# Keys of the first batch through a hardware queue in float32, cast on the chip, and a new order of all steps

## The chip, the cores and the metric

The kernel runs on one core of a Trainium2 chip. The metric is the device time of one execution in microseconds. The core has five engines with instruction queues of their own: PE (TensorE, matmuls), DVE (VectorE), ACT (ScalarE), POOL (GpSimd) and SP (SyncE). Each works through its own queue in order, and semaphores hold an instruction back until its inputs are there. Transfers between memory and the core's own memory (SBUF) run on 16 DMA engines. They are fed by three queues here: POOL's, the software queue, which can also change a type on the way, and the hardware queues of SP and ACT. Matmul results land in PSUM, which holds eight tiles of this kernel at a time.

## What is computed

Attention over a small learned memory, and then a channel mix with weights. All shapes are fixed: 8 batches, 8 heads, 576 tokens, head size 64, 32 memory slots, and a mix of 512 to 1024 and back.

```python
a = softmax(phi, axis=2)                              # over the 576 tokens
k_m = einsum('bhsm,bhsd->bhmd', a, k)                 # 32 slots a head
v_m = einsum('bhsm,bhsd->bhmd', a, v)
attn = softmax(matmul(q, k_m^T) / 8)                  # over the 32 slots
x = matmul(attn, v_m)                                 # heads side by side: 512 wide
x_prev = x moved down by one token (zeros first)
xk = mu_k * x + (1 - mu_k) * x_prev
xr = mu_r * x + (1 - mu_r) * x_prev
kk = maximum(xk @ w_k, 0)
out = sigmoid(xr @ w_r) * ((kk * kk) @ w_v)
```

## The kernel before

The whole order of work is written out by hand in `PLAN`, a list of words, and each word is one step. The kernel's last loop goes through the words and records the instructions of each step, so a word's place sets its instructions' places in the queue of every engine that it uses. Nothing moves them afterwards. A word has a batch number (`0:s0`), or one of these heads:

- `p:` a load through POOL's queue: `p:q:0h` is the second half (heads 4 to 7) of batch 0's queries, `g` the first half, `p:k:1` all keys of batch 1, `p:wk:0-4` half of the weights `w_k`. `PRE` has the loads that come before everything else; `id` there builds the identity matrix on POOL.
- `c0:` to `c8:` keys of one group of tokens (L533): four matmuls of `w_k` with `xk`, relu on ACT (L540) or, with a `v` at the end, on DVE (L538), and the square on DVE (L545). Group 0 is batch 0 in two parts, `a` (320 tokens) and `b` (256); the others have 512.
- `g:` gate matmuls of one tile of 128 tokens (L561) and an exp on ACT (L566), `sg:` the rest of the sigmoid for two tiles (L572, L573), `o:` the output (L587), its product with the gate on DVE (L589) and the store on SP's queue.

The steps of a batch, in the order in which data flows through them:

- `exp`: the exponential of phi on ACT (L216); for batch 0 in two halves, `exp0` and `exp1`.
- `z`: sums of it over the tokens on PE (L240), and their reciprocal on DVE (L243).
- `kg0`, `kg1` for batch 0, `k`, `v`, `kv` later: `k_m` and `v_m` on PE (L230). A half needs its keys, and its half of `exp`.
- `nk` (DVE, L267) or `ak` (ACT, L265): the scaling of `k_m`. `tk`: its transposition on PE (L295) and the copy back on DVE (L300).
- `q0`, `q1`: the two halves of the queries transposed on DVE (L313). `s`, or `s0` and `s1`: scores on PE (L328) and their exponential on ACT (L333). Either part of the scores reads both halves of the queries.
- `l`, `h`, `y` or `fe`, `fs`, `fo`, `w`: two ways to divide by the softmax's sum. The first sums on PE (L343), takes a logarithm and an exponential on ACT (L348, L353) and multiplies on DVE (L377). The second does all on DVE.
- Batches 0 and 1 fold mu into `v_m` (`nm`, `nk0`, `nr0`, L425 and L437) and get `xk` and `xr` by matmuls (`mk`, `mr`, L286) with four copies each, two on ACT and two on DVE (L454). Later batches form `x` (`x0`, `x1`, copies on ACT, L389) and mix it on DVE (`dd`, `k0d`, `r2d`, L401 to L415), or in part on ACT (`r0e`, L412).

`mub` and `mu` need the two mu rows, `mu2`, which SP loads at the very start (L117, L118). `mub` spreads them by two matmuls on PE (L191) and two copies on DVE (L194, L195) for batches 0 and 1. `mu` is a small transposition (L199) with a DVE instruction (L200), for the later batches. `busyN` are N matmuls on zeros whose result nobody uses (L184): fillers, while PE has nothing else.

Phi of batch 0 comes through ACT's queue (L105). Queries, keys and values are float32 in memory and bfloat16 in SBUF, so POOL's queue casts them on the way; each has two buffers (`qs`, `kvs`), used by even and odd batches.

Of the kernel before, what the change touches and what calls it, by code (L numbers as in the profile page):

```python
# [10 lines left out]
F32 = mybir.dt.float32  # L11
# [5 lines left out]


PLAN = [
    "0:busy17 0:exp0 p:q:0g 0:q0 0:mub 0:exp1 0:z 0:kg0 0:busy7_1 p:k:0h 0:kg1 0:busy2_2 0:nk p:q:0h 0:q1 0:tk",  # L20
    "0:busy3_3 0:s0 p:v:0g 0:s1 0:busy2_4 0:l1 0:h1z 0:l3 0:busy2_5 p:v:0h 0:y1 0:vg1 0:h3z 0:y3 0:l0 0:l2 0:vg0",
    "0:busy3_6 0:nm1 0:nm0 0:h2z 0:y2 0:h0z p:wk:0-4 0:y0 0:mk1 0:mk0 c0:2b 0:mr1 c0:1b p:wk:4-8 c0:5a c0:0av p:phi:1",
    "c0:4bv c0:5bv 1:exp c0:4a c0:3a 0:mr0 1:z c0:3b c0:2a p:wr:0-4 c0:6b g:3 c0:0b c0:7av g:2 sg:1 0:mu p:k:1 1:k",
    "1:nk p:q:1 1:q1 1:q0 g:1 g:0 1:tk c0:1av 1:s c0:7bv c0:6a 1:l0 p:wv:0-2 1:h0z o:3a 1:l3 1:l2 1:h2z 1:l1 1:y0",
    "o:2a 1:h3z 1:y2 p:v:1 1:v 1:nk1 1:nk0 1:nr1 1:y3 1:h1z 1:y1 sg:0 o:0a p:wv:2-4 o:1a 1:mk0 p:phi:2 o:1b 2:exp",
    "o:3b 1:mk1 1:nr0 o:2b p:v:2 p:k:2 c1:2 c1:5v 1:mr1 c1:7 c1:4 2:z 2:kv 2:nk 1:mr0 p:q:2 2:q0 c1:3 2:av 2:tk 2:q1",
    "c1:1 c1:0 c1:6v 2:s o:0b 2:fe 2:fs 2:fo 2:w0 p:phi:3 3:exp p:v:3 p:phi:4 g:4 g:6 2:w1 g:5 3:z sg:2 o:4 o:5 4:exp",
    "2:x1 p:k:3 3:kv 3:nk 4:z 3:av p:q:3 2:x0 3:q1 g:7 3:q0 3:tk g:8 p:k:4 2:dd 2:k0d 3:s 2:k2d sg:3 o:6 3:l0 3:l3",
    "3:l2 2:r0d 3:l1 3:r0z 3:w0 o:7 3:r1z 3:w1 c2:4 c2:6 p:v:4 p:phi:5 c2:1 5:exp 2:r2d c2:3 c2:0 p:q:4 4:q1 4:kv",
    "4:av 4:q0 3:x0 c2:2 c2:5 4:ak p:q:5 c2:7 5:z 3:x1 3:dd 3:k2d g:11 g:10 sg:5 4:tk 5:q0 3:k0d 5:q1 g:9 o:11 o:10",  # L30
    "sg:4 o:8 3:r0e 4:s p:k:5 p:phi:6 p:v:5 5:kv 4:fe 4:fs 5:av 5:ak 3:r2e o:9 5:tk c3:7 6:exp c3:0 c3:3 4:fo c3:5",
    "5:s 5:fe 4:w1 4:w0 g:13 c3:2 c3:4 g:14 5:fs c3:1 p:q:6 4:x1 c3:6 6:z 5:fo 4:x0 4:dd 4:k0d 4:k2d 5:w1 g:15 p:q:7",
    "sg:7 g:12 sg:6 p:k:7 o:12 o:14 5:w0 p:phi:7 o:15 7:exp p:k:6 c4:5 c4:1 o:13 6:q1 7:z 6:q0 7:q0 4:r2e p:v:7 5:x1",
    "c4:7 p:v:6 6:kv 7:kv 7:nk 6:ak 6:av 5:x0 5:dd 4:r0e c4:6 6:tk c4:2 5:k0d g:16 g:17 5:k2d c4:0 c4:4 c4:3 7:q1 6:s",
    "6:fe g:19 6:fs 6:fo c5:3 g:18 c5:6 c5:1 sg:8 c5:5 7:nv 6:w0 6:w1 c5:0 5:r2e c5:2 o:17 sg:9 o:19 6:x1 o:16 c5:4v",
    "c5:7 6:x0 6:dd 6:k0d g:21 6:k2d 7:tk g:20 sg:10 o:21 o:20 5:r0e o:18 c6:7 c6:6 7:s 7:fe g:22 7:fs 7:fo c6:4 g:23",
    "sg:11 7:w1 g:26 c6:1v 7:w0 c6:5 6:r2e c6:3 c6:0 c6:2 o:23 7:x1 o:22 6:r0e 7:x0 7:dd g:25 7:k0d 7:k2d g:24 sg:12",
    "o:25 7:r2d g:27 sg:13 o:27 o:26 c7:1v o:24 c7:2 c8:2 c7:3 c8:3 c8:4v c7:0 c7:5v 7:r0e c8:5v g:29 c7:7 c7:6v",
    "c8:6v g:32 g:33 sg:16 g:28 c7:4v c8:0v sg:14 c8:7v o:28 c8:1 o:29 g:31 g:30 sg:15 o:30 o:33 o:31 g:34 g:35 sg:17",
    "o:34 o:32 o:35",  # L40
]

PRE = "k:0g id:"
SUMS = ()


NJ = 9
# [3 lines left out]
def kernel(  # L51
# [13 lines left out]
    nc = tc.nc  # L65
    B, H, S, D = q.shape
# [18 lines left out]
    work = ctx.enter_context(tc.sbuf_pool(name="work", bufs=2))  # L85
# [14 lines left out]
    def rows(src):  # L100
        return src.rearrange("h s d -> (h s) d").rearrange("(a p j) d -> p a (j d)", a=HH, j=NJ)

    def load_phi(b, eng):
        ph = ld.tile([128, HH, NJ, M], F32, name="ph", tag="ph")
        eng.dma_start(out=ph.rearrange("p h j m -> p h (j m)"), in_=rows(phi[b]))  # L105
        loads[b] = ph
# [5 lines left out]
        nc.gpsimd.dma_start(out=dst[r].rearrange("p h j d -> p h (j d)"), in_=rows(src)[r])  # L112

    load_phi(0, nc.scalar)
    nc.vector.memset(zeros, 0.0)  # L115
    mu2 = const.tile([2 * ND, 128], F32, name="mu2")
    nc.sync.dma_start(out=mu2[:ND, :], in_=moe_mu_k.rearrange("(a b) -> a b", b=128))  # L117
# [12 lines left out]
    def preload(word):  # L130

        what, _, part = word.partition(":")
        if what in weights:
            dst, src = weights[what]
            f0, f1 = (int(x) * 128 for x in part.split("-"))
            nc.gpsimd.dma_start(out=dst[:, :, f0:f1], in_=src[:, :, f0:f1])
        elif what == "id":
            make_identity(nc, identity)
        else:
            n = int(part[0])  # L140
            if what == "phi":
                load_phi(n, nc.gpsimd)
            else:
                dst = qs[n % 2].rearrange("p (h j) d -> p h j d", j=NJ) if what == "q" else kvs[n % 2][:, "kv".index(what)]
                src = {"q": q, "k": k, "v": v}[what][n]
                if part[1:] in ("g", "h"):
                    gs = slice(0, 2) if part[1] == "g" else slice(2, 4)
                    nc.gpsimd.dma_start(out=dst[:, gs].rearrange("p h j d -> p h (j d)"), in_=rows(src)[:, gs])  # L148
                elif part[1:]:
                    load_parity(dst, src, ROWS["ab".index(part[1])])  # L150
                else:
                    load_rows(dst, src)

    for word in PRE.split():
        preload(word)
# [46 lines left out]
    def attention(b):  # L202
        st = {}

        def ps_tile(shape, dtype, name):
            return psum.tile(shape, dtype, name=name, tag="ps", bufs=8)
# [5 lines left out]
        x0 = b * S % RING  # L212
        kv5, em = kvs[b % 2], ems[b % 2]

        def exp_phi(hs=slice(0, None)):
            nc.scalar.activation(em[:, :, hs].rearrange("p j h m -> p h j m"), loads[b][:, hs], AF.Exp)  # L216

        def ekv(parts, cs=(0, 1), gs=range(HH)):

            def go():  # L220
                w = parts.stop - parts.start
                kvps = st.get(("kvps", parts.start), {})
                kvps.update({c: ps_tile([128, w, D], F32, "kvps") for c in cs if c not in kvps})
                st["kvps", parts.start] = kvps
                for i in range(w):
                    st.setdefault("kv"[parts.start + i], {}).update({c: kvps[c][:, i, :] for c in cs})
                for j in range(NJ):
                    for g in gs:
                        for c in cs:
                            nc.tensor.matmul(kvps[c][g * M:(g + 1) * M], lhsT=em[ROWS[c], j, g, :],  # L230
                                             rhs=kv5[ROWS[c], parts, g, j, :],
                                             start=j == 0, stop=j == NJ - 1,
                                             skip_group_check=True)
            return go
# [68 lines left out]
        def q_tile():  # L303
            if "qT" not in st:
                st["qT"] = work.tile([128, HH, NJ * PB, 2], BF16, name="qT", tag="qT", bufs=2)
            return st["qT"]

        def turn_q(rows_, gs):

            def go():  # L310
                dst = q_tile()[rows_, gs].rearrange("p g n h -> p (g n h)")
                src = qs[b % 2][rows_, gs.start * NJ:gs.stop * NJ].rearrange("p n d -> p (n d)")
                nc.vector.transpose(dst.bitcast(U32), src.bitcast(U32))  # L313
            return go
# [127 lines left out]
        def mixed(w, hf):  # L442

            def go():
# [7 lines left out]
                for i in range(ND):  # L452
# [5 lines left out]
        steps = {"exp": exp_phi, "kv": ekv(slice(0, 2)), "k": ekv(slice(0, 1)), "v": ekv(slice(1, 2)),  # L458
                 "z": esum, "nk": norm_k(), "nv": norm_v(), "ak": norm_k(by_act=True), "av": norm_v(True), "tk": tr_k(), "s": scores((0, 1)), "mu": load_mu, "mub": load_mu_b,
                 "zr": sum_rows}  # L460
        steps.update(fe=fold_e, fs=fold_sum, fo=fold_out)
        for i in range(2):
            steps[f"q{i}"] = turn_q(slice(0, 128), slice(2 * i, 2 * i + 2))
            steps[f"qh{i}"] = turn_q(ROWS[i], slice(0, HH))
            steps[f"kg{i}"] = ekv(slice(0, 1), gs=range(2 * i, 2 * i + 2))
            steps[f"vg{i}"] = ekv(slice(1, 2), gs=range(2 * i, 2 * i + 2))
            steps[f"nm{i}"] = norm_both(i)
            steps[f"k{i}c"] = ekv(slice(0, 1), (i,))
            steps[f"v{i}c"] = ekv(slice(1, 2), (i,))
            steps[f"exp{i}"] = lambda i=i: exp_phi(slice(2 * i, 2 * i + 2))  # L470
            steps[f"hn{i}"] = norm_k((i,))
            steps[f"ha{i}"] = norm_k((i,), by_act=True)
            steps[f"ht{i}"] = tr_k((i,))
            steps[f"hc{i}"] = tr_k((i,), nc.scalar.copy)
            for w in range(2):
                steps[f"n{'kr'[w]}{i}"] = norm_mu(w, i)
# [127 lines left out]
    for n, word in enumerate(" ".join(PLAN).split()):  # L604
        who, _, name = word.partition(":")
# [38 lines left out]
```

## Time and profile before

| | us |
|---|---|
| median of 3 runs (lowest, highest) | 205.98 (205.87, 206.58) |
| the profiled execution | 206.46 |
| its span, first to last instruction | 204.7 |
| PE busy | 192.6 (94%) |
| DVE busy | 155.8 (76%) |
| ACT busy | 152.3 (74%) |
| POOL busy | 30.0 (15%) |
| fillers on PE, 36 matmuls | 10.4 |

Busy times can't be read as one limit, since PE waits at the start and hardly ever later. The span falls into a head without keys to compute (to 19.5 us), a long stretch in which all five engines and the DMA engines work at once, and a tail of 4.9 us after PE's last matmul. Loads run from 2 us to 109.6 us almost without a pause. In the profile's tables "PEld" is the weight load of a matmul, which overlaps PE, and a line such as L533 is a line of the kernel before.

### The profile page before, as it was taken

Reading aid. Unit: us, or ns where it says so; the run is one execution under the profiler, and the core shown is the slowest. Engines: PE = TensorE matmul, PEld = TensorE weight load, DVE = VectorE, ACT = ScalarE, POOL = GpSimd, SP = SyncE. Lnnn points to the kernel's source line nnn. Section 1 sums busy time; section 2 is a strip of 40 time slices with the busy share of each in tenths; the row PEclk is TensorE's granted clock in tenths of the full one; section 3 lists DMA queues with packets and bytes.
Section 4 is the critical chain, followed back from the end, with each engine's and each line's share of the span. In section 5 each row is a group of like instructions: output and inputs, shape, how many; then the busy total and the mean of one; then the engine's idle time right before and its main releaser. Section 6 shows DMA issues by size and latency. Waiting matters only on the chain.

```text
span 204.7 us, 5403 instructions
## 1 busy us (share of the span) xinstructions
PE 192.6 (94%) x2197; PEld 98.5 (48%) x2197; DVE 155.8 (76%) x362; ACT 152.3 (74%) x295; POOL 30.0 (15%) x45
## 2 busy tenths in 40 slices
PE   8868999898898999999999999999999999999990
PEld 3424767655444445444446764444444444444450
DVE  2147968775898999999999999979797987762330
ACT  3137869855598999999899988976899926495350
POOL 7743321142021401080000000000000000000000
PEclk9999999999999999999999999999999999999997
DMA  6999999999999999999997300060603162004334
GB/s 158 162 207 260 211 203 206 270 231 277 277 221 222 293 232 271 216 154 258 284 208 163 86 3 0 0 154 5 155 0 74 33 153 52 0 0 106 87 80 140
DMA packets 24520, 31.28 MB, mean 153 GB/s; under 512 B 1960, under 2 KB 19632, under 8 KB 24496
## 3 DMA queue, kind: packets, MB, share of 16 engines
q0 software_dynamic: 17392, 20.91, 54.7%
q1 hardware_dynamic: 6336, 9.18, 17.7%
q10 hardware_dynamic: 768, 0.85, 1.4%
q8 instruction: 17, 0.28, 0.5%
q14 instruction: 7, 0.06, 0.1%
HBM read 38.28 MB, written 9.44 MB: 233 GB/s over the span
## 4 chain that ended last, share of the span: by engine, by line
PE 68%; DMA 14%; ACT 10%; DVE 2%; POOL 2%; issue 1%; POOLq 0%; ACTq 0%
PE pk L533 27%; PE pv L587 23%; DMA q<-in_q_dram 14%; PE pr L561 12%; PE kvps L230 2%; ACT e L333 2%; ACT sg L572 2%; PE scps L328 1%; PE nops L286 1%; DVE qT L313 1%; ACT sg L573 1%; PE mxps L286 1%; ACT lz L353 1%; ACT sg L566 1%; POOL kv L148 1%
## 5 line engine op out<-in xcount | busy, mean ns | idle before, releaser
L533 PE MATMUL pk<-xkT,wk 128*128 128x512 bf16 (+4 forms) x352 | 67.6, 340 | 0.2 <-ACT xkT L454 0.2
L587 PE MATMUL pv<-wv,sq 128*128 128x512 bf16 (+1 forms) x328 | 66.6, 353 | 0.6 <-ACT sg L572 0.6
L533 PEld LDWEIGHTS <-wk 128*128 128x128 bf16 x352 | 33.0, 98 | 28.6 <-issue 0.8
L587 PEld LDWEIGHTS <-sq 128*128 128x128 bf16 x328 | 31.3, 98 | 30.6 <-issue 1.2
L540 ACT ACTIVATE rl<-pk 128x512 bf16<-128x512 f32 (+3 forms) x61 | 33.8, 570 | 13.8 <-PE pk L533 13.0
L545 DVE TENSOR_TENSOR sq<-rl 128x512 bf16<-128x512 bf16 (+5 forms) x104 | 31.7, 336 | 8.1 <-ACT rl L540 7.0
L561 PE MATMUL pr<-wr,xrT 128*128 128x512 bf16 x144 | 34.9, 379 | 0.0
L589 DVE TENSOR_TENSOR o<-sg,pv 128x512 f32<-128x512 f32 (+1 forms) x41 | 24.6, 617 | 13.4 <-ACT sg L573 9.6
L566 ACT ACTIVATE sg<-pr 128x512 f32<-128x512 f32 x36 | 21.3, 624 | 11.0 <-PE pr L561 11.0
L561 PEld LDWEIGHTS <-xrT 128*128 128x128 bf16 x144 | 13.2, 98 | 14.7 <-issue 0.7
L573 ACT ACTIVATE sg<-sg 128x1024 f32<-128x1024 f32 x18 | 19.0, 1057 | 0.6
L572 ACT ACTIVATE sg<-sg 128x1024 f32<-128x1024 f32 x18 | 19.0, 1057 | 0.4
L333 ACT ACTIVATE e<-scps 128x288 bf16<-128x288 f32 x32 | 10.5, 418 | 10.0 <-PE scps L328 9.9
L313 DVE STREAM_TRANSPOSE qT<-q 128x576 uint32<-128x576 uint32 x16 | 11.9, 763 | 7.8 <-DMA q<-in_q_dram 7.8
L389 ACT CAST x<-nops 128x256 bf16<-128x256 f32 (+1 forms) x48 | 15.8, 435 | 0.9 <-PE nops L286 0.9
L377 DVE TENSOR_TENSOR atn<-e,lz 128x576 bf16<-128x576 bf16 (+2 forms) x20 | 12.2, 631 | 3.0 <-ACT lz L353 2.9
L538 DVE TENSOR_SCALAR rl<-pk 128x512 bf16<-128x512 f32 (+3 forms) x19 | 11.3, 594 | 2.5 <-PE pk L533 2.4
L412 ACT ACTIVATE mu_d<-diff,mu 128x576 bf16<-128x576 bf16 x18 | 13.0, 780 | 0.0
L216 ACT ACTIVATE em<-ph 128x1152 bf16<-128x1152 f32 (+1 forms) x9 | 9.4, 1055 | 2.6 <-DMA ph<-in_phi_dram 2.6
L184 PE MATMUL idle<-zeros 128*128 128x512 bf16 x36 | 10.4, 426 | 1.0 <-DVE zeros L115 1.0
L401 DVE TENSOR_TENSOR diff<-x 128x1024 bf16<-128x1024 bf16 (+1 forms) x18 | 8.9, 552 | 2.2 <-ACT x L389 2.2
L230 PE MATMUL kvps<-kv,em 64*32 64x128 bf16 (+1 forms) x720 | 8.2, 210 | 2.3 <-DMA kv<-in_k_dram 2.3
(69 smaller groups left out, 159.0 us busy)
## 6 DMA issues: line engine op xcount, KB each, us to landing
out_dram<-o SPq DMA_DIRECT2D x61, 128.0 KB, 2.4
ph<-in_phi_dram POOLq DMA_DIRECT2D x7, 576.0 KB, 16.2
kv<-in_k_dram POOLq DMA_DIRECT2D x7, 576.0 KB, 16.7
q<-in_q_dram POOLq DMA_DIRECT2D x7, 576.0 KB, 18.0
kv<-in_v_dram POOLq DMA_DIRECT2D x7, 576.0 KB, 19.5
out_dram<-o SPq DMA_DIRECT2D x18, 64.0 KB, 5.7
wk<-in_moe_w_k_dram POOLq DMA_DIRECT2D x2, 512.0 KB, 12.5
wv<-in_moe_w_v_dram POOLq DMA_DIRECT2D x2, 512.0 KB, 20.0
```

The lines of the kernel that those rows point to most:

```text
L313: nc.vector.transpose(dst.bitcast(U32), src.bitcast(U32))
L333: nc.scalar.activation(e[:, hf], pss[c, hf], AF.Exp, scale=scale)
L389: nc.scalar.copy(st["x"][:, i, sl], pss[i])
L533: nc.tensor.matmul(pk[:, p0 - lo:p1 - lo], lhsT=wk_sb[:, di, fi * 128:(fi + 1) * 128], rhs=xk_T[:, di, p0 % RING:p0 % RING + p1 - p0], sta ...
L540: nc.scalar.activation(rl, pk, AF.Relu)
L545: nc.vector.tensor_mul(sq[:, fi, p:p + p1 - p0], rl[:, part], rl[:, part])
L561: nc.tensor.matmul(pr, lhsT=xr_T[:, di, c0:c0 + 128], rhs=wr_sb[:, di, :], start=(di == 0), stop=(di == ND - 1))
L566: nc.scalar.activation(sg[:, t % 2], pr, AF.Exp, scale=-1.0)
L572: nc.scalar.activation(gated[p], gated[p], AF.Ln, bias=1.0)
L573: nc.scalar.activation(gated[p], gated[p], AF.Exp, scale=-1.0)
L587: nc.tensor.matmul(pv[:, cols], lhsT=sq[:, fi, p:p + 128], rhs=wv_sb[:, fi, cols], start=(fi == 0), stop=(fi == NF - 1))
L589: nc.vector.tensor_mul(o[:, cols], gated[t // 2][:, t % 2, cols], pv[:, cols])
```

## The change

Three parts.

1. Batch 0's keys don't come through POOL's queue any more. SP loads them as float32, in two halves, into two work buffers that share the three slots of `x`. The step `cast_k` then converts them to bfloat16: in quarters, `c00` and `c01` of the first half, `c10` and `c11` of the second, an `a` at the end for ACT and a `d` for DVE. SP's two mu rows are loaded after them.
2. POOL's first load is the first half of the queries, in place of the first half of the keys.
3. Every word of `PLAN` has a new place. The same steps are there for all batches; other variants are used for some: 10 of batch 0's 16 key steps have their relu on DVE where 6 had it, 18 of the other 64 where 13 had it, and 6 of 12 `r` mixes of batches 2 to 7 are on DVE where 3 were. Fillers go from 36 to 30.

```diff
 PLAN = [
-    "0:busy17 0:exp0 p:q:0g 0:q0 0:mub 0:exp1 0:z 0:kg0 0:busy7_1 p:k:0h 0:kg1 0:busy2_2 0:nk p:q:0h 0:q1 0:tk",
-    "0:busy3_3 0:s0 p:v:0g 0:s1 0:busy2_4 0:l1 0:h1z 0:l3 0:busy2_5 p:v:0h 0:y1 0:vg1 0:h3z 0:y3 0:l0 0:l2 0:vg0",
-    "0:busy3_6 0:nm1 0:nm0 0:h2z 0:y2 0:h0z p:wk:0-4 0:y0 0:mk1 0:mk0 c0:2b 0:mr1 c0:1b p:wk:4-8 c0:5a c0:0av p:phi:1",
...
-    "o:2a 1:h3z 1:y2 p:v:1 1:v 1:nk1 1:nk0 1:nr1 1:y3 1:h1z 1:y1 sg:0 o:0a p:wv:2-4 o:1a 1:mk0 p:phi:2 o:1b 2:exp",
-    "o:3b 1:mk1 1:nr0 o:2b p:v:2 p:k:2 c1:2 c1:5v 1:mr1 c1:7 c1:4 2:z 2:kv 2:nk 1:mr0 p:q:2 2:q0 c1:3 2:av 2:tk 2:q1",
-    "c1:1 c1:0 c1:6v 2:s o:0b 2:fe 2:fs 2:fo 2:w0 p:phi:3 3:exp p:v:3 p:phi:4 g:4 g:6 2:w1 g:5 3:z sg:2 o:4 o:5 4:exp",
-    "2:x1 p:k:3 3:kv 3:nk 4:z 3:av p:q:3 2:x0 3:q1 g:7 3:q0 3:tk g:8 p:k:4 2:dd 2:k0d 3:s 2:k2d sg:3 o:6 3:l0 3:l3",
...
+    "0:busy13 0:mub 0:mu 0:busy5_1 0:c01a 0:exp0 0:c00d 0:kg0 0:exp1 0:c10d 0:z 0:c11a 0:kg1 0:busy3_2 0:nk 0:q0 0:tk",
+    "0:busy2_3 p:q:0h 0:q1 0:s1 0:s0 p:v:0g 0:vg0 0:busy1_4 p:v:0h 0:l2 0:busy1_5 0:h2z 0:l1 0:vg1 0:nm1 0:l3 0:h3z",
+    "0:nm0 0:y3 0:y2 0:l0 0:busy5_6 0:h0z 0:y0 0:h1z 0:y1 0:mr0 0:mk0 0:mk1 p:wk:0-4 c0:3a c0:2a c0:1av c0:0av",
...
+    "p:v:2 1:nk0 1:l0 1:l1 c0:3bv 1:l3 1:h0z p:phi:2 1:y0 1:h3z 1:y3 1:h1z 1:y1 1:l2 1:h2z 1:y2 g:3 o:1b o:0b p:k:2",
+    "p:q:2 1:mk1 1:mk0 1:mr0 c1:0 c1:5v c1:3v sg:1 1:mr1 2:exp p:phi:3 c1:6v 3:exp o:2a o:1a c1:1v o:3b 2:z 2:kv 2:nk",
+    "2:nv o:0a 2:tk 2:q0 2:q1 c1:2v c1:7v c1:4 2:s g:4 3:z p:phi:4 4:exp 2:fe 2:fs 2:fo 2:w0 p:v:3 2:w1 o:3a g:5 sg:2",
+    "o:2b 4:z g:6 o:5 o:4 2:x1 p:k:3 3:kv 3:ak p:q:3 p:v:4 3:q1 2:x0 3:av 3:q0 g:7 3:tk g:8 3:s 2:dd 2:k0d 2:k2d sg:3",
...
 ]
 
-PRE = "k:0g id:"
+PRE = "q:0g id:"
...
     load_phi(0, nc.scalar)
+    k0 = []
+    for gs in (slice(0, 2), slice(2, 4)):
+        k0.append(work.tile([128, 2, NJ, D], F32, name="k0f", tag="x", bufs=3))
+        nc.sync.dma_start(out=k0[-1].rearrange("p h j d -> p h (j d)"), in_=rows(k[0])[:, gs])
     nc.vector.memset(zeros, 0.0)
     mu2 = const.tile([2 * ND, 128], F32, name="mu2")
     nc.sync.dma_start(out=mu2[:ND, :], in_=moe_mu_k.rearrange("(a b) -> a b", b=128))
...
+        def cast_k(gs, eng):
+
+            def go():
+                dst, src = kv5[:, 0, gs], k0[gs.start // 2][:, gs.start % 2:gs.start % 2 + gs.stop - gs.start]
+                if eng == "a":
+                    nc.scalar.copy(dst, src)
+                else:
+                    nc.vector.tensor_copy(dst, src)
+            return go
...
+            for e in "ad":
+                steps[f"c{i}{e}"] = cast_k(slice(2 * i, 2 * i + 2), e)
+                for h in range(2):
+                    steps[f"c{i}{h}{e}"] = cast_k(slice(2 * i + h, 2 * i + h + 1), e)
```

## The prediction

> **What bounds the kernel now.** I read the busy time by stage first, then the chain of waits, then the first 13 us in order of time, and last what the matmul engine waited for in the middle. By stage (columns: stretch, its length, busy us and instructions of PE, PEld, DVE, ACT, POOL, granted clock, DMA share, GB/s):
>
> ```profile
> 5.20:13.20 8.00, 5.95 (x105) 2.98 (x103) 3.06 (x8) 0.69 (x2) 5.47 (x8) 1.00 1.14 178
> ...
> 18.73:65.80 47.07, 44.33 (x780) 26.94 (x779) 36.67 (x93) 36.52 (x79) 9.87 (x14) 1.00 1.22 239
> 65.80:199.80 134.00, 133.87 (x1179) 65.17 (x1179) 111.99 (x245) 109.00 (x202) 8.18 (x11) 1.00 0.55 119
> ```
>
> From 65.80 to 199.80 PE is busy 133.87 of 134.00 us. The change takes no matmul of that stretch away, so time can only be won or lost before 65.80, or lost after it. In the chain of waits the head hangs on the queries of batch 0 (start, us, what):
>
> ```profile
> 4.02 8.15 DMA q<-in_q_dram
> 12.16 0.02 issue
> 12.19 0.78 DVE qT L313
> 12.97 0.19 DVE kmT L300
> 13.15 0.04 issue
> 13.20 0.52 PE scps L328 x32
> ```
>
> The scores (L328) start at 13.20, the first weighted values are mixed at 18.73, the first keys (L533) run at 19.51. The same stretch in order of time (start, us, engine, line):
>
> ```profile
> 0.74 0.37 SPq L117 DMA_DIRECT2D mu<-in_moe_mu_k_dram  x1
> ...
> 1.40 0.15 PEld L184 LDWEIGHTS <-zeros 128*128 128x128 bf16 x1 [0.27 <-issue]
> 1.82 0.15 PEld L184 LDWEIGHTS <-zeros 128*128 128x128 bf16 x1 [0.28 <-issue]
> ...
> 6.15 0.71 PE L191 MATMUL mub<-mu,sel 8*128 8x128 f32 x4
> ...
> 10.00 0.39 DVE L194 COPY mu_m<-mub 128x256 f32<-128x256 f32 x1
> 10.31 0.41 DVE L195 TENSOR_SCALAR mu_m<-mub 128x256 f32<-128x256 f32 x1
> ...
> 10.74 0.44 PE L230 MATMUL kvps<-kv,em 64*32 64x64 bf16 x36 [1.17 <-DMA kv<-in_k_dram]
> ...
> 11.26 0.61 DVE L267 TENSOR_SCALAR kbd<-kvps,rz 128x128 bf16<-128x128 f32 x2 [0.47 <-PE kvps L230]
> ```
>
> The mu rows are SyncE's first transfers and serve `mub` early. Between 36 and 66 us PE waits four times for batch 2 and 3's loads or what follows them, and once for ACT (0.6):
>
> ```profile
> PE scps L328 <- DVE kmT L300: 0.9, 2, 0.6
> PE kvps L230 <- DMA kv<-in_k_dram: 0.8, 1, 0.8
> ...
> PE scps L328 <- DVE qT L313: 0.4, 1, 0.4
> ```
>
> As gaps between PE's instructions these are 0.66 (47.07), 0.28 (52.72), 0.36 (53.33) and 0.58 us (65.21): 1.88 us that a later head can use up for nothing.
>
> **The change, part by part.** *Loads.* POOL loses the two key halves (0.82 and 0.72 us of issue); SyncE gains two (0.37 each, the mu row's) and issues mu after them. The casts need no more HBM bytes. New is that three queues pull at once: phi on ACT's from 1.85 us (its first packet), keys on SyncE's from about 1.7 (where the first mu packet ran), POOL's from 3.6 (its first packet before). How queues share is seen at 66 to 68 us:
>
> ```profile
> q0 software_dynamic: 187, 0.25, 63.1%
> q1 hardware_dynamic: 187, 0.31, 48.2%
> ```
>
> Packet for packet. A phi packet (1152 bytes) takes 51 ns in the packet records, an uncast 4608-byte one 178, so a key row of 2304 about 93 (estimate between the two); a cast 1152-byte packet takes 107. Each of the 16 engines has 32 phi packets, 32 key packets (16 a half) and 16 for each q half. Up to 3.6 us phi and keys alternate: 1.9 us at a share of 1.05 (106% stood at 4 to 8 us) over 144 ns is 13.9 pairs. The other 18.1 go in threes with POOL's: 18.1 x 251 ns / 1.06 = 4.3 us. Phi and the second key half end together at 7.9 and land some 0.4 later, as phi did: **T = 8.3 us**. If no POOL packet came between, 32 x 51 ns and 32 x 93 ns are 4.6 us, at the software queue's 1.2 over 3.8 after 1.7, plus 0.4: 5.9; at the 0.87 that phi's queue held from 3 to 4 us, 9.9. So the last phi is 3.7 us later than now (exp started at 4.64), the last keys 2.4 sooner (10.74).
>
> *Mu behind keys.* On SyncE's queue mu now follows 1.18 MB, so it lands at T, not near 3. By the order of the changed program, DVE stands at mu's three copies before it comes to its key casts, and PE at `mub` with five fillers, kg0, z and kg1 behind it. ACT's first cast stands before exp0, but its half lands near 4.7, before phi. From T: handoff 0.05, mub 0.71, handoff 0.10, copies 0.39 + 0.41 + 0.17 (L200's row); two casts of 128x576 on DVE. Those are not in the trace: L158's cast of 8 elements took 158 ns and L165's of 256 took 319, 0.65 ns an element, so 0.53 for 576; bounds 0.37 (`mu_d`, same size in SBUF) and 0.71 (L454's slope from PSUM). I take 0.53, a cast within SBUF too. Then kg1 0.45 (+0.05), nk 0.61 (+0.08), q0 0.78, kmT's remainder 0.19, q1 0.78 (now in front of both score halves), handoff 0.05. Sum 5.88: scores at **14.2, against 13.20: +1.0**. ACT's casts and the two exps (0.63 each, from T) end at T + 1.9 and hide under DVE's chain; with mu early they would be the bound. [...] No float32 SBUF copy of this size is in this trace.
>
> *After the scores* the ACT chain (4 e, 4 Ln, 4 Exp) is the same instructions: +0. Then mr0 stands before mk0 and mk1, where mk1 and mk0 led. First keys must wait for four rounds of copies (2 x 0.43 us on ACT, 2 x 0.48 on DVE each for xrT and xkT, 320 wide), about 1.8 us, under which 64 mix matmuls (1.3 us) run: PE idle 0.5 where it had 0.17, **+0.3** (0 to +0.6).
>
> *Batch 0's keys.* Ten relus instead of six are DVE's, 4 x 0.45 = 1.8 us more between 22 and 37, where DVE had about 3.5 of 16 us free: **+0.2** (0 to +0.8). *Batch 1's mix.* Now mk1, mk0, mr0 stand together ahead of c1:0; DVE owes two outputs (0.42 each) and four copies (1.8) first, PE has 0.5 of mr0 to cover it. Idle of about 1.2 against the present 0.55 (37.76): **+0.6** (-0.5 to +1.2).
>
> *The middle.* PE comes to 2:kv, 2:s and 3:s about 2.1 us late; 2:kv with 0.4 and 2:s with 0.9 us less matmul work ahead of it. The four waits for loads are then over: **-1.88**. That needs loads no later than now; the same bytes start in three queues, so they are rather 0 to 1.5 us sooner. 3:exp stands before 2:s on ACT and waits for phi 3 (landed 53.94): e of batch 2 comes some 2 us later than now, hidden under g4 to o4 (8.7 us of PE). *Late.* PE's six dropped fillers stood in waits: 0. DVE gets about 3 us more work in the last 134, in which it has 22 free: **+0.2** (0 to +1). POOL's later issues stay in their depth of backlog (14 to 20 us to landing): 0. The float32 keys lie in two of three "x" buffers that nothing uses until batch 2's x at 61 us: 0.
>
> Sum: 1.0 + 0.3 + 0.2 + 0.6 - 1.88 + 0.2 = **+0.4**. The profiled execution takes 206.46 (span 204.70 and 1.76 around it), so 206.9; the median of the runs shown is 205.98, lower by 0.48, so **206.4** there.
>
> **Rivals.**
> (A) Slower: the keys land late. One mechanism, three queues taking turns and mu last: at T = 9.9 scores start at 15.8, +1.6 over the sum: 208.0. It decides from T = 8.9 on, when the sum passes +1.03 (0.5%). For it: the fair turns; against: the hardware queues start 1.9 us ahead of POOL's.
> (B) Slower: the fillers end at about 5.3 and PE then stands until T. In the trace the first fillers come 0.42 us apart, from 3.9 on 0.20: PE begins at half rate. If it falls back, mub, kg1, tk and the scores double (+1.9): 208.3. Against: after the present 1.15 us of idle the fillers still ran 0.20 apart. [...]
> (C) Slower: the new order itself stalls PE after 66 us, because DVE or ACT, 97 and 96% busy between 64 and 112, come late: +1 to +2 in place of +0.2, so 207.4 or so.
> (D) Faster: mu isn't held back and the keys land near 7. Then T + 4.9 (exps, ACT's cast, kg1, nk, q0, kmT, q1) gives 11.9, -1.3; with no extra stall in batch 1 the limit is batch 3's queries, up to 1.5 us sooner: 204.5. For it: nothing else in the chain is late; against: transfers of one queue start in order.
> (E) The change does nothing in the end: 3:s waits for batch 3's queries at 65.8 as now: 206.0.
>
> **Numbers.** Forecast 0.35 and E 0.05 make "within 0.5%" (1.03 us, about what a measurement of this kernel can tell) 0.40; A 0.22, B 0.08 and C 0.12 make slower 0.42; D 0.18 faster. The forecast's own range is 205.4 to 207.0 (cast and stall bounds each way). The range reaches to D's 204.5 below and past A to B's 208.3 above.
>
> **What would show it.** `mub` at 8 to 9 us right behind the last key packet; DVE's casts after mu_m; scores near 14.2; no wait at 2:kv, 2:s, 3:s. It is wrong if `mub` runs at about 5 (D), if fillers after T are 0.4 apart (B), or if PE idles after 66 us by more than 0.5 (C).

## The result and the profile after

| | before | after |
|---|---|---|
| median (lowest, highest; 13 runs each) | 206.12 (205.78, 206.95) | 207.40 (206.54, 207.87) |
| ratio, 95% interval | | 1.0053 (1.0036 to 1.0071) |
| the profiled execution, its span | 206.46, 204.7 | 207.81, 205.7 |
| scores of batch 0, most of them | 13.20 | 17.11 |
| first keys of the mix | 19.51 | 24.06 |
| PE's last matmul | 199.78 | 201.40 |
| from the first keys to there | 180.27 | 177.34 |

The changed kernel is slower by about half a per cent. In the profiled executions the first keys come 4.55 us later. The stretch behind them is 2.93 shorter and the tail 0.62, so 1.00 of span is left. Another 0.35 lies outside the span (2.14 us in place of 1.79), which makes up the 1.35 between the two executions; no run shows what it is. Runs more than 1.5% above the fastest of their kernel are left out of the ratios; that concerns two of the seven of e5_loads_alone below.

Lines of the changed kernel have moved: `mub` is now L195, `mu` L203, the fillers L188, the key casts L227 (ACT) and L229 (DVE), the sums with keys and values L244, the scaling L281, the queries L327, the scores L342, the softmax's sums L357, the mix L300, the keys L551.

The chain of waits of the changed kernel, its head (start, us, what):

```profile
2.21 7.11 DMA mu<-in_moe_mu_r_dram
9.32 0.14 issue
9.46 1.19 PE mub L195 x4
10.65 0.01 PE psmu L203
10.66 2.24 PE idle L188 x5
12.90 0.60 PE kvps L244 x29
...
17.11 0.48 PE scps L342 x26
...
22.12 0.62 PE mxps L300 x24
...
24.13 5.25 PE pk L551 x40
```

The queries no longer lead. The second mu row, 2 KB, is under way from 2.21 to 9.32. `mub` follows it at once, and then come five fillers of 0.45 us each ahead of the first key sums. The same stretch in order of time (start, us, engine, line; in brackets the idle time before and what ended it):

```profile
5.20 0.67 ACT L227 CAST kv<-k0f 128x576 bf16<-128x576 f32 x1 [2.64 <-DMA k0f<-in_k_dram]
...
6.76 1.25 ACT L220 ACTIVATE em<-ph 128x576 bf16<-128x576 f32 x2 [0.89 <-DMA ph<-in_phi_dram]
...
9.46 1.19 PE L195 MATMUL mub<-mu,sel 8*128 8x128 f32 x4 [3.17 <-DMA mu<-in_moe_mu_r_dram]
...
10.68 0.42 DVE L198 COPY mu_m<-mub 128x256 f32<-128x256 f32 x1 [6.68 <-PE psmu L203]
...
11.43 0.82 DVE L229 CAST kv<-k0f 128x576 bf16<-128x576 f32 x2
```

The first half of the keys was there at 5.20, and ACT cast its quarter then. DVE, whose quarter of the same half was as ready, stood 6.68 us at mu's copies and cast it at 11.43. `mub`'s matmuls take 1.19 in place of 0.71. By stage (stretch, length, busy us and instructions of PE, PEld, DVE, ACT, POOL, granted clock, DMA share, GB/s), the clock shows why:

```profile
6.30:9.40 3.10, 0.00 (x0) 0.00 (x0) 0.00 (x0) 1.58 (x3) 1.44 (x2) 0.96 1.16 257
9.40:17.11 7.71, 7.27 (x103) 3.85 (x103) 4.01 (x11) 0.34 (x1) 3.87 (x5) 0.57 1.19 244
```

PE has no matmul for 3.1 us, and then a granted clock of 0.57 up to the scores. The trace's clock records say 0.5 from 9.13 to 15.95. Behind the head PE waits for something only once between 24 and 66 us; the four waits for loads are gone (engine, line, releaser, us in all, times, longest):

```profile
PE zps L357 <- ACT e L347: 0.5, 1, 0.5
```

### The profile page after: what moved, and what is told of

Read it like the earlier page. It is cut to its first block, busy times and chain, and to the rows that moved or that the text cites. A ratio compares the mean times of both kernels' runs of the same rounds, so it can differ in the third digit from the quotient of the medians.

```text
span 205.7 us, 5377 instructions
## 1 busy us (share of the span) xinstructions
PE 193.7 (94%) x2171; PEld 100.3 (49%) x2191; DVE 160.9 (78%) x377; ACT 145.4 (71%) x284; POOL 28.5 (14%) x43
## 4 chain that ended last, share of the span: by engine, by line
PE 86%; ACT 5%; DMA 3%; DVE 1%; issue 1%; SPq 1%
PE pk L551 30%; PE pv L605 29%; PE pr L579 15%; DMA mu<-in_moe_mu_r_dram 3%; PE kvps L244 3%; PE mxps L300 2%; PE idle L188 2%; PE nops L300 2%; ACT e L347 2%; PE scps L342 1%; PE zps L254 1%; ACT sg L584 1%; DVE atn L391 1%; PE mub L195 1%; ACT sg L591 1%
## 5 line engine op out<-in xcount | busy, mean ns | idle before, releaser
L551 PE MATMUL pk<-xkT,wk 128*128 128x512 bf16 (+4 forms) x346 | 66.9, 340 | 0.4
L551 PEld LDWEIGHTS <-wk 128*128 128x128 bf16 x352 | 32.9, 98 | 28.0 <-issue 0.8
L558 ACT ACTIVATE rl<-pk 128x512 bf16<-128x512 f32 (+3 forms) x52 | 29.3, 585 | 19.1 <-PE pk L551 17.4
L556 DVE TENSOR_SCALAR rl<-pk 128x512 bf16<-128x512 f32 (+3 forms) x28 | 16.3, 584 | 0.3 <-PE pk L551 0.2
L188 PE MATMUL idle<-zeros 128*128 128x512 bf16 x30 | 11.7, 541 | 1.0 <-DVE zeros L119 1.0
L327 DVE STREAM_TRANSPOSE qT<-q 128x576 uint32<-128x576 uint32 x16 | 11.8, 759 | 0.0
L428 DVE TENSOR_SCALAR mu_d<-diff,mu 128x576 bf16<-128x576 bf16 x36 | 11.6, 364 | 0.1
L105 POOL DMA_DIRECT2D ph<-in_phi_dram x7 | 5.3, 762 | 35.0 <-ACT em L220 18.2
```

Source lines behind the costliest of these rows:

```text
L188: nc.tensor.matmul(ps.rearrange("p (a b) -> p a b", b=128), lhsT=zeros, rhs=zeros.unsqueeze(1).to_broadcast([128, blocks, 128]), start=Tru ...
L551: nc.tensor.matmul(pk[:, p0 - lo:p1 - lo], lhsT=wk_sb[:, di, fi * 128:(fi + 1) * 128], rhs=xk_T[:, di, p0 % RING:p0 % RING + p1 - p0], sta ...
L556: nc.vector.tensor_scalar_max(rl, pk, 0.0)
L558: nc.scalar.activation(rl, pk, AF.Relu)
```

## The experiments

Each kernel ran beside the kernel before on the same chip (its medians there 205.95, 206.05 and 206.12). "First keys" and "last matmul" are from the profiled execution of each.

| run | median (lowest, highest) | ratio (95%) | first keys | last matmul | between |
|---|---|---|---|---|---|
| old order: e4_late9 | 205.96 (205.37, 206.28) | 0.9994 (0.9984–1.0004) | 20.46 | 198.98 | 178.52 |
| e9_old_late | 206.11 (205.82, 206.40) | 0.9996 (0.9987–1.0005) | 21.80 | 199.18 | 177.38 |
| e5_loads_alone | 206.93 (205.09, 207.68) | 1.0029 (0.9993–1.0065) | 24.50 | 202.36 | 177.86 |
| new order: e3_order_alone | 204.24 (203.89, 204.57) | 0.9909 (0.9889–0.9929) | 21.01 | 198.24 | 177.23 |
| e10_new_late | 207.39 (207.11, 207.71) | 1.0059 (1.0043–1.0074) | 24.02 | 201.30 | 177.28 |
| e6_order_warm | 204.39 (203.92, 205.21) | 0.9921 (0.9894–0.9948) | 20.52 | 197.95 | 177.43 |
| and new loads: e1_mu_first | 204.37 (204.12, 204.98) | 0.9920 (0.9897–0.9943) | 21.23 | 198.57 | 177.34 |
| e2_fillers | 207.82 (206.23, 208.61) | 1.0085 (1.0053–1.0116) | 22.57 | 199.78 | 177.21 |
| e7_mub_late | 204.33 (203.28, 205.13) | 0.9910 (0.9878–0.9941) | 20.01 | 197.54 | 177.53 |
| e8_mub_late_warm | 204.11 (204.06, 204.28) | 0.9905 (0.9890–0.9920) | 20.65 | 198.03 | 177.38 |
| e11_late_warm3 | 203.40 (203.24, 203.55) | 0.9862 (0.9846–0.9878) | 19.70 | 197.44 | 177.74 |
| e12_late_warm0 | 203.35 (203.31, 204.28) | 0.9871 (0.9853–0.9890) | 20.07 | 197.28 | 177.21 |

**The mu rows ahead of the keys.** The changed kernel with SP's four loads in another order:

```diff
+    mu2 = const.tile([2 * ND, 128], F32, name="mu2")
+    nc.sync.dma_start(out=mu2[:ND, :], ...)
+    nc.sync.dma_start(out=mu2[ND:2 * ND, :], ...)
     k0 = []
...
-    mu2 = const.tile([2 * ND, 128], F32, name="mu2")
-    nc.sync.dma_start(out=mu2[:ND, :], ...)
-    nc.sync.dma_start(out=mu2[ND:2 * ND, :], ...)
```

> The changed kernel with SyncE's two mu rows issued ahead of the two key halves; nothing else is moved. Theory (mu behind 1.18 MB of keys on the same queue holds PE and DVE, and the idle that follows takes the clock): mub at 5.3 to 6.3 instead of 9.46, no PE idle above 2 us before the scores, no half clock from 9 to 16, scores at 12.6 to 13.2 instead of 17.1, and 205.2 us (204.6 to 205.9), below the kernel before, with waits for loads of batches 2 and 3 back in the middle. Rival (the new order of steps is itself the cost): scores may come early, but the time stays at 206.8 or more.

Measured: 204.37, 1.5% below the changed kernel. `mub` ran at 5.21, though the keys landed later than in the changed kernel (6.4 and 10.2 in place of 5.18 and 9.05). The first keys of the mix came 2.83 us sooner (21.23 against 24.06) and PE's last matmul 2.83 sooner (198.57 against 201.40). So the place of 4 KB behind 1.18 MB costs 3.0 us, with what it adds of half clock, and in the new order the head sets the end one for one. The time is below the 204.6 to 205.9 that I expected, since no wait for a load came back in the middle. The head was not as expected either: PE stood 2.02 us for the second half of the keys, a half clock followed (0.50 from 10.51 to 13.93), and the scores came at 13.99.

**More fillers under the wait.**

```diff
-    "0:busy13 0:mub 0:mu ...
+    "0:busy28 0:mub 0:mu ...
```

> The changed kernel with 28 fillers in place of 13 ahead of mub, so that PE has work until the mu rows land. Theory (the half clock from 9 to 16 us is a second cost on top of the late mu rows): clock 1.00 from about 6 us on, mub 0.7 in place of 1.19 us, scores at 15.3 in place of 17.1, 206.6 us, and all runs within 0.4 us of each other near the fastest runs of the changed kernel (206.5 to 206.9). Rival (the clock only marks the wait and costs nothing of its own): scores still past 16.5, median 207.2 to 207.6.

Measured: 207.82, no better than the changed kernel; the theory's 206.6 holds for three runs of eight. The runs fall into two groups: three of 206.23 to 206.60 at a mean granted clock of 0.997 or more, five of 207.67 to 208.61 at 0.987 or less. The profiled one is of the first group: no half clock, `mub` 0.68 us, most scores at 14.68, 2.43 sooner than in the changed kernel. So the fillers hold the clock up in some runs only. Where they do, 1.9 to 2.2 us over e1_mu_first's 204.37 remain for the late start, though e1_mu_first has a half clock in its head and these have none. A stop of 0.80 us of PE, which e8_mub_late_warm shows too, is among it.

**The new order alone.** The new `PLAN` with keys through POOL's queue, the mu rows first and no casts:

```diff
-    "0:busy13 0:mub 0:mu 0:busy5_1 0:c01a 0:exp0 0:c00d 0:kg0 0:exp1 0:c10d 0:z 0:c11a 0:kg1 ...
+    "0:busy13 0:mub 0:mu 0:busy5_1 0:exp0 0:kg0 0:exp1 0:z 0:kg1 ...
...
-PRE = "q:0g id:"
+PRE = "k:0g id: q:0g k:0h q:0h"
...
```

> The new order of steps with batch 0's keys through POOL's queue as before (first half of keys, identity, first half of queries, then the other halves) and mu first on SyncE's; no casts on the chip. Theory (the order costs little: 0.3 for the mix, some tenths elsewhere): scores near 13.4, waits for loads in the middle as before, 206.3 us (205.9 to 206.8). Rival (the order is the cost): 207.0 or more.

Measured: 204.24, faster than before by 0.9%, where I had expected 206.3 and the rival 207.0. The first keys come 1.50 us later than before (21.01), and yet the last matmul 1.54 sooner: the stretch between them is 3.04 shorter. No wait for a load is left in it.

Two things besides those waits are in the gain. Of the 3.04, some 0.6 us has only changed its place: 64 matmuls of batch 0's mix run ahead of the first keys in the new order, 40 in the old (16 of them take 0.42 us behind the first keys, so 24 some 0.6, an estimate). And the tail behind the last matmul is 3.93 us, 0.97 shorter; it is 4.6 to 4.9 in all kernels of the old order and 3.9 to 4.3 in all of the new one, and no run shows why.

The loads of batches 2 and 3 land sooner (keys of batch 2 at 46.43 in place of 47.70, its queries at 49.33 for 51.64, batch 3's at 62.38 for 64.11). But they do so as well in e4_late9 and e9_old_late below, which have the old order (45.97 and 46.10, 50.08 and 49.94, 62.44 and 63.07). So the kernel before had its loads late in the execution that was profiled, which took 206.46 against a median of 206.12, and how much sooner the new order brings them is not shown.

The order is the part of the change that pays, and it owes nothing to the keys: e1_mu_first, which adds the new key loads to it, has the same time.

**The new loads alone**, in the old order, with SP's keys behind the mu rows:

```diff
-    "0:busy17 0:exp0 p:q:0g 0:q0 0:mub 0:exp1 0:z 0:kg0 0:busy7_1 p:k:0h 0:kg1 0:busy2_2 0:nk p:q:0h ...
+    "0:busy17 0:c01a 0:exp0 0:mub 0:exp1 0:z 0:c00d 0:kg0 0:busy7_1 0:c10d 0:c11a 0:kg1 0:busy2_2 0:nk 0:q0 p:q:0h ...
...
-PRE = "k:0g id:"
+PRE = "q:0g id:"
...
```

> The old order of steps with batch 0's keys in float32 through SyncE's queue behind the mu rows, queries first on POOL's, and four cast quarters on ACT and DVE. Theory (the loads themselves help the head a little, and all later loads come sooner): second key half at about 9.2, scores at 12.7 in place of 13.2, waits for loads of batches 2 and 3 shorter by up to 1 us, 205.5 us (205.0 to 206.0). Rival (float32 keys delay phi and the first queries so that nothing is won): 206.1 or more.

Measured: 206.93, spread over 205.09 to 207.68, so no clear difference from before, and not the 205.5 expected. The trace is of a longer execution (208.78), and what follows holds for that one alone: ACT's first cast waits for keys until 9.2, ahead of exp, and PE stands 3.75 us; the fillers after that come 0.43 us apart, as they do in the changed kernel at its clock of 0.5. The first keys come at 24.50, 4.99 later than before, and the last matmul only 2.58 later. A late head in the old order is in part taken up.

**How much a late head costs in either order.** Only fillers are added, in front of batch 0's scores: 9 and 15 in the old order, 15 in the new one of e3_order_alone.

```diff
-    "0:busy3_3 0:s0 p:v:0g ...
+    "0:busy12_3 0:s0 p:v:0g ...
```

> The kernel before with nine more fillers (12 in place of 3, some 0.2 us each, so 1.9 us) in front of the first half of the scores; nothing else differs. Theory: the order before stands up to 1.88 us between 47 and 66 us for loads of batches 2 and 3, and a later head is used up there for nothing: scores near 14.8 in place of 13.20, the end within 0.3 us of before's 205.95, so 205.7 to 206.5, and the gaps at the scores and the key sums of batches 2 and 3 are smaller than before's 0.66, 0.28, 0.36 and 0.58. Rival: the loads are issued by the same late steps, so their arrival moves along and the time is 207.3 to 207.9.

```diff
-    "0:busy3_3 0:s0 p:v:0g ...
+    "0:busy18_3 0:s0 p:v:0g ...
```

> The kernel before with 15 more fillers (18 in place of 3) in front of the first half of the scores; e4_late9's 9 moved the scores and the first keys by 0.95 us and the time by nothing. Theory: with 15 the first keys come some 2.2 us later than before's 19.51, of which the waits for loads between 47 and 66 us take up to 1.88: the time is 206.0 to 206.8, at most 0.7 above before. Rival: e4_late9's 0.95 was hidden by something else, and 2.2 us of head cost 1.5 or more: 207.5 or more.

```diff
-    "0:busy2_3 0:q1 0:s1 0:s0 p:v:0g ...
+    "0:busy17_3 0:q1 0:s1 0:s0 p:v:0g ...
```

> The same 15 fillers in the new order alone (e3_order_alone, 204.24), in front of its scores. Theory: the new order has no waits for loads left, so what the fillers add to the head (some 2 us at the first keys) stands in the time in full: 206.0 to 206.8, 1.8 to 2.5 above e3_order_alone, while the same edit costs the order before at most 0.7. Rival: the new order absorbs as much as the old: 204.9 or less.

Measured: in the old order the first keys come 0.95 and 2.29 us later and the time stays (205.96 beside 206.05, 206.11 beside 206.12). In the new order they come 3.01 later, the last matmul 3.06 later and the time is 3.15 higher (207.39 against 204.24); that is more than the 1.8 to 2.5 that I expected, and a half clock fell on the fillers (10.91 to 14.32; the mean clock is 0.992 in all four runs). The stretch from the first keys to the last matmul, in the kernel before, in e9_old_late and in e10_new_late (columns as above):

```profile
19.51:199.78 180.27, 177.61 (x1926) 91.62 (x1925) 148.25 (x337) 145.10 (x279) 17.89 (x24) 1.00 0.72 149
```
```profile
21.80:199.18 177.38, 176.83 (x1926) 91.81 (x1925) 148.19 (x337) 144.92 (x279) 17.14 (x23) 1.00 0.72 148
```
```profile
24.02:201.30 177.28, 176.60 (x1906) 91.62 (x1901) 151.55 (x346) 136.03 (x264) 16.41 (x22) 1.00 0.71 146
```

PE's idle time in it (length less busy) is 2.66, 0.55 and 0.68 us. The old order stands for loads unless its head is late; the new one has nothing to stand for. (The 2.66 is of the execution with late loads; that the old order has room rests on the times, medians of ten runs and more.) The rows of the table bear it out: in the new order the stretch has 177.2 to 177.7 whether it begins at 19.70 or at 24.02, in the old one it shrinks from 180.27 to 178.52, 177.38 and 177.86 as its start moves from 19.51 to 20.46, 21.80 and 24.50. In e9_old_late one wait for a load is left between 24 and 90 us:

```profile
PE kvps L230 <- DMA kv<-in_v_dram: 0.4, 1, 0.4
```

**`mub` out of the way.** The changed kernel, its loads as they are, with two words moved:

```diff
-    "0:busy13 0:mub 0:mu 0:busy5_1 0:c01a ...
+    "0:busy13 0:busy5_1 0:c01a ...
-    "0:busy2_3 p:q:0h 0:q1 0:s1 0:s0 p:v:0g ...
+    "0:busy2_3 p:q:0h 0:q1 0:s1 0:s0 0:mub 0:mu p:v:0g ...
```

> The changed kernel with the two words mub and mu moved from the front to behind the scores of batch 0; SyncE's transfers stay in the changed kernel's order, the keys first and the mu rows after them, landing near 9.3. Theory: the cost of the late mu rows is that mub, its three copies on DVE and with them every cast and key sum stand behind them, and not the transfers themselves: casts at 5.3 (first half) and 9.1 (second half), scores at 12.6 to 13.2 in place of 16.43, and 204.2 (203.7 to 204.8). Rival: what is late in the changed kernel is the second half of the keys and all that follows from it, so moving mub wins only its own 1.2 us and DVE's 1.2: 205.9 or more.

Measured: 204.33, 3.1 us below the changed kernel, and near the 204.2 expected. Of this 0.35 lies outside the span (1.79 us again, as before). In order of time (e7_mub_late):

```profile
5.53 0.46 DVE L229 CAST kv<-k0f 128x576 bf16<-128x576 f32 x1 [1.52 <-DMA k0f<-in_k_dram]
...
9.30 0.46 DVE L229 CAST kv<-k0f 128x576 bf16<-128x576 f32 x1 [3.31 <-DMA k0f<-in_k_dram]
...
12.73 0.50 PE L342 MATMUL scps<-qT,kmT 32*32 32x288 bf16 x28 [0.38 <-DVE qT L327]
...
13.15 0.71 PE L195 MATMUL mub<-mu,sel 8*128 8x128 f32 x4
```

Both halves are cast as soon as they land, and the scores come 4.38 us sooner than in the changed kernel (12.73 against 17.11), with the mu rows landing no sooner. So what cost was the late transfer's place in front of PE's and DVE's work, as the theory said, and not the keys: the rival's 205.9 falls. The runs again are of two kinds: 203.28 to 203.73 at a mean clock of 0.996 or more, 204.92 to 205.13 at 0.987 or less.

**Holding the clock.** Fillers between z and the second key sums, in e3_order_alone (where two value steps also move back by two places) and in e7_mub_late:

```diff
-    ... 0:exp1 0:z 0:kg1 0:busy3_2 ...
+    ... 0:exp1 0:z 0:busy6_9 0:kg1 0:busy3_2 ...
-    ... 0:h2z 0:l1 0:vg1 0:nm1 0:l3 0:h3z",
-    "0:nm0 0:y3 0:y2 0:l0 0:busy5_6 ...
+    ... 0:h2z 0:l1 0:l3 0:h3z 0:l0 0:vg1 0:nm1",
+    "0:nm0 0:y3 0:y2 0:busy5_6 ...
```

> The new order alone (e3_order_alone, 204.24) with 6 more fillers between batch 0's z and kg1, where PE stood 1.85 us, and with the two v steps vg1 and nm1 two places later, behind l3 and l0, since PE stood 0.88 us there for values that landed at 16.10. Theory: the head sets the end one for one in the new order, because nothing later waits for loads; without the half clock from 11.36 to 14.77 and with that stall filled, scores at 12.2, the first mix at 18.2 to 18.7 in place of 19.07, and 203.5 (203.0 to 204.1). Rival: the head is bound by DVE's and ACT's chain behind the scores, and the order's end by something else: 204.1 or more.

```diff
-    ... 0:c10d 0:z 0:c11a 0:kg1 ...
+    ... 0:c10d 0:z 0:busy6_9 0:c11a 0:kg1 ...
```

> e7_mub_late with 6 more fillers between batch 0's z and kg1, so that PE isn't idle for more than 1 us while the second half of the keys is loaded and cast. Theory: PE's clock then stays at 1.0 through the scores, and against e7_mub_late it is 0.3 to 0.7 us faster: 203.7 (203.2 to 204.4). Rival: the half clock falls on work that waits for DVE and ACT anyway, and the time is e7_mub_late's within 0.2.

Measured: e6_order_warm 204.39, no gain, so the theory's 203.5 failed; e8_mub_late_warm 204.11, all four runs within 0.22, but only 0.22 below e7_mub_late's median, where the theory had 0.3 to 0.7. The profiled runs of both have no half clock in the head (mean clock 1.000 and 0.995). But PE stopped in the sums of the values, for 0.79 and 0.75 us, at a place where e7_mub_late doesn't stop. The chain of waits of e8_mub_late_warm there:

```profile
14.91 0.37 PE kvps L244 x34
15.28 0.75 issue
16.03 0.20 PE kvps L244 x2
```

The stop names no engine and no transfer of data. In the queue of instructions one packet of 16 KB lies shortly ahead of it, from 13.64 to 14.58 (a window of 0.1 us, queue, kind: packets, MB, share):

```profile
q8 instruction: 1, 0.02, 58.4%
```

In all four runs that stop like this, PE goes on 1.37 to 1.47 us after that packet's end (e2_fillers 16.40 to 17.87, e6_order_warm 14.88 to 16.25, e8_mub_late_warm 14.58 to 16.03, e11_late_warm3 14.31 to 15.75). In all four it stops at the same place of its queue, with 445 to 447 matmuls and weight loads done, and in no kernel here does the 448th start sooner than 1.3 us after the end of that packet. That PE waits there for its own instructions is the reading that fits; no record of the traces names what it waits for. Two last kernels test it with half as many fillers, and with six that take the place of six others ahead of the stop:

```diff
-    ... 0:z 0:busy6_9 0:c11a ...
+    ... 0:z 0:busy3_9 0:c11a ...
```

> e8_mub_late_warm with 3 more fillers than e7_mub_late between z and kg1, in place of 6. In e8_mub_late_warm, e6_order_warm and e2_fillers PE stood 0.75 to 0.80 us in the value sums of batch 0 with nothing that the profile names but issue, each time until 1.4 us after the end of a packet of 16 KB in the queue of instructions; in e7_mub_late it didn't, because it came to the same number of instructions later. Theory: the fillers ahead bring PE to the end of the instructions that it has loaded sooner than the next 16 KB arrive, so half as many fillers stand half as long: a wait of 0.2 to 0.5 there, first mix at 18.2 to 18.5, 203.5 to 203.9. Rival: the stop belongs to the edit itself: 0.75 again, 204.1.

```diff
-    ... 0:c11a 0:kg1 0:busy3_2 0:nk 0:q0 0:tk",
-    "0:busy2_3 ... 0:vg0 0:busy1_4 p:v:0h 0:l2 0:busy1_5 0:h2z ...
+    ... 0:c11a 0:kg1 0:nk 0:q0 0:tk",
+    "0:busy1_3 ... 0:vg0 p:v:0h 0:l2 0:h2z ...
```

> e8_mub_late_warm with its 6 fillers between z and kg1, and 6 others taken away (all 3 ahead of nk, 1 of 2 ahead of the scores, 1 and 1 among the softmax's sums), so that as many instructions stand in front of the value sums as in e7_mub_late. Theory: no stop for instructions, no half clock before the scores: 203.3 to 203.7 in all runs, the fastest of these kernels. Rival: the taken fillers kept the clock up, a half clock comes after 10 us in some runs: 204 to 205.

Measured: 203.40 and 203.35, 1.4% and 1.3% below the kernel before and 1.9% below the changed kernel. With three fillers the stop is still there but shorter, 0.44 us, as expected:

```profile
PE zps L357 <- issue: 0.4, 1, 0.4
```

With as many instructions ahead as in e7_mub_late there is no such stop at all. In that kernel a half clock came from 13.71 to 17.12 in the profiled run and cost it little; one run of five took 204.28, at the lowest mean clock (0.978).

## Why the prediction came out as it did

The forecast was 206.4, within half a per cent of before; it came out just beyond, at 207.40, inside the range. Both signs of the sum were right and neither size was. That the total came so near is luck, since two errors of about 3 us took each other away. The head, scores and mix together, was to cost 1.3 us and cost 4.55. All behind it was to win 0.9 and won 3.55, of which 0.62 lies in the tail; the sum had no term for the tail, and none for the 0.35 outside the span.

- *Scores +1.0.* They came 3.91 later (17.11 against 13.20). **This is the step that failed**: the head's "T = 8.3" and "T + 5.88". The last keys landed at 9.05 and the second mu row at 9.32, so T was 1.0 too early. From T to the first score matmuls it took 7.11 us (9.32 to 16.43), 1.2 more than worked out, and the rest of the scores waited for the second half of the queries until 17.11, 0.68 more. e2_fillers shows what the half clock does there: without it the scores come 5.38 after `mub`'s start (9.30 to 14.68) and with it 7.65. I had worked out 5.83 from there, so at full clock the chain of work was no longer than I thought. What failed is T, by 1.0, and the half clock, which the sum put at nothing and rival B at a chance of 0.08.
- *How the queues share.* "Packet for packet" was read from a stretch with one hardware queue beside POOL's. The two hardware queues did not alternate: from 1.5 to 3 us SP's keys have 99 packets and ACT's phi 14, from 3 to 5 us phi 334 and keys 173. These are the queues of the changed kernel from 1.5 to 3 and from 3 to 5 us (packets, MB, share of 16 engines):

```profile
q1 hardware_dynamic: 99, 0.23, 61.0%
q10 hardware_dynamic: 14, 0.02, 6.4%
```
```profile
q10 hardware_dynamic: 334, 0.38, 54.9%
q1 hardware_dynamic: 173, 0.36, 46.2%
```

  So phi landed at 6.74, not with the last keys, and POOL's first packet came at 5.29 and not at 3.6. A key packet took 109 ns in the mean and 94.5 in the median, where I estimated 93 from medians, so the packet's price was right and the turns were not.
- *DVE's casts, 0.53 each.* 0.41 measured (0.82 for the two), inside the bounds.
- *Mu behind keys, in front of DVE's casts:* right, in place and order (`mub` right behind the last keys, the casts behind mu's copies), and e1_mu_first and e7_mub_late show that this alone makes the change slower: 3.0 and 3.1 us.
- *Mix order +0.3:* +0.36 from the first mix to the first keys (1.58 before, 1.94 after); another +0.28 lies between the scores and the mix, where I had 0. *Batch 0's keys +0.2, batch 1's mix +0.6, late DVE +0.2:* they didn't come; PE's one wait between 24 and 66 us is 0.5 long, as long as before's 0.55 at 37.76, which is gone.
- *The four waits, -1.88.* They went, and more with them: 2.93 for the whole stretch, some 0.6 of it mix matmuls that now stand ahead of the first keys. (The first of the four, at 47.07, is 0.77 us in the trace and not 0.66, so they were 1.99.) For the old order the reading was right and e9_old_late shows it: 2.29 us of late head for nothing. But in the new order the waits are gone without a late head: in e11_late_warm3 the first keys come at 19.70, and PE waits for no load behind them. I wrote that the loads are "rather 0 to 1.5 us sooner" and did not draw the conclusion that the waits could go by the change itself. Each microsecond of a late head then had to be paid (e10_new_late).
- *Rivals.* A and B came together, each in part. A, keys late: they landed at 9.05 and the mu rows at 9.32, past its 8.9. B, half clock: it followed PE's 3.17 us of idle time (0.5 from 9.13 to 15.95); I had worked out 3.0 us of it and gave B a chance of 0.08, when the longest idle seen was the 1.17 of the kernel before. The changed kernel's runs lie in two groups, five of 206.54 to 206.90 at a mean clock of 0.991 to 0.992 and eight of 207.26 to 207.87 at 0.978 to 0.983; their medians, 206.71 and 207.64, are 0.9 us apart. C did not come, D (204.5) is what e1_mu_first and e7_mub_late make true by other edits, and E's limit by batch 3's queries is gone.

What stays open: why the two hardware queues were served in blocks; how far the half clock alone lengthens the changed kernel, as no kernel of it was made that never has one; why the new order has no waits for loads, and why its tail is shorter.

## What to carry to other kernels

A small transfer that early work waits for belongs ahead of the big ones on its queue, or the work that needs it belongs behind whatever does not: moving two words was worth 3.1 us here, more than twice the loss. When a wait looks like free room for a late start, ask first whether the same change removes that wait by another way; a plain delay in both versions tells it in two runs. Judge the parts of a change apart: this one held an order worth 0.9%, and was slower as a whole. With the key loads, `mub` out of the way and the clock held (0.995 to 1.000 in the mean of its four runs) it came to 1.4% (e11_late_warm3's 0.9862 beside e3_order_alone's 0.9909); how much of the 0.5% between is the key loads' is not shown, as `mub` was not moved without them.

## What the runs showed of the hardware

- **The clock halved after 3.41 us in which PE had been busy for 0.58 to 1.95 us.** In the profiled runs the half clock lasted 3.41 us (10.51 to 13.93 in e1_mu_first, 11.36 to 14.77 in e3_order_alone, 13.71 to 17.12 in e12_late_warm0) or twice that (9.13 to 15.95 in the changed kernel), at another place in each. The 3.41 us just before had PE busy for 0.58 us in the changed kernel, 0.84 in e1_mu_first, 1.55 in e3_order_alone and 1.95 in e12_late_warm0, where PE was never idle for more than 0.74 us at a time. But 1.74 in e6_order_warm (15.51 to 18.93), 1.95 in e7_mub_late (15.80 to 19.22) and 2.06 in the kernel before (7.25 to 10.67, with 1.17 us of idle up to 10.74) did not bring it. And in the changed kernel it went on for a second 3.41 us, though PE had been busy for 3.08 of the first. So neither the longest idle time nor PE's busy time decides alone, and what does stays open. Here are the 3.41 us before and the 3.41 us of the half clock in e3_order_alone (the column before the DMA share is the clock):

```profile
7.95:11.36 3.41, 1.55 (x50) 0.91 (x50) 0.93 (x4) 0.00 (x0) 1.97 (x3) 1.00 1.19 197
11.36:14.77 3.41, 3.41 (x75) 1.34 (x76) 1.40 (x3) 1.25 (x4) 1.48 (x2) 0.50 1.22 208
```
- **PE stopped at one place of its queue, until 1.4 us after a packet of instructions.** With three to fifteen more fillers in the head PE stopped there for 0.44 to 0.80 us, until 1.37 to 1.47 us after the end of a packet of 16 KB in the queue of instructions, in four kernels. In e10_new_late, whose fillers ran in part at half clock (10.91 to 14.32), PE came to that place 3.9 us after the packet's end and did not stop. In e8_mub_late_warm the stop is 0.75 us of the chain of waits (15.28 to 16.03).
